# Agent attention and a PReLU feed-forward on one core: the step of a four-copy rounding and the step of one unit's split are changed

## The chip, the core and the metric

The kernel runs on one core of a Trainium2 chip. The metric is the device time of one execution in microseconds; three runs of the kernel before gave 957.25, 957.55 and 958.12 us, so the median is 957.55 us. The core has a matrix engine (TensorE, PE in the rows; PEld is its loading of weights), a vector engine (DVE), a scalar engine (ACT), a general engine (POOL, GpSimd) and a queue that issues DMAs (SP). Each engine works through its own list of instructions in order and waits at a semaphore where another engine's result is needed. PE writes to PSUM; everything else lies in SBUF.

## What is computed

Two batches of 12480 queries, keys and values of width 128 and 49 agents are attended in two stages, and the result goes through a feed-forward with 2048 hidden units:

```
a2k = softmax(scale * agents @ k^T);  agent_v = a2k @ v
q2a = softmax(scale * q @ agents^T);  x = q2a @ agent_v        # 24960 x 128
h = x @ w_in;  g = max(h, 0) + alpha * min(h, 0)
out = g @ w_out
```

Everything is float32 outside. The kernel works in a rounded 32-bit format on PE and splits numbers into a high and a low part (names that end in h and l) to keep the accuracy.

## The kernel before

**Tiling.** The 24960 rows of the output are cut into 52 groups of 480; a group takes 8 steps, so the main loop has 416 steps, numbered from 0. Step s does three things in this order: `g1(s + 2)`, then whatever a plan has put at step s, then `g2(s)`. `g1(s)` makes two blocks of 128 hidden units for its group in PSUM (tile `h`, two buffers: h of step s takes the place of h of step s - 2), as six matmuls in three pairs; ACT then writes `rh = relu(h)`, rounded (line 1077), and DVE writes `rl = relu(h) - rh` (line 1078). `g2(s)` adds these two blocks, times `w_out`, to the group's sum (tile `acc`), as twelve matmuls in six pairs (line 1094). A pair of matmuls works on the two halves of PE's rows side by side. So PE's list can't go past `g1(s + 2)` before DVE has finished `rl` of step s, which reads the buffer that g1(s + 2) overwrites. In the orders below, `rl111` is the `rl` of step 111, and so on; the profile leaves these numbers out.

**The plan.** All other work of the main loop is put at steps by tables of numbers at the head of the file; at one step, work stands in the order in which the code put it in. The scheduler moves nothing: the order written is the order on each engine. Three kinds of such work matter here.

*The query chain.* For each pair of groups, DVE turns the queries (`qt`, line 884), ACT and DVE split them (`qh` 895, `ql` 902), PE makes the logits (921), ACT takes them (`qs`, 929), a DMA swaps the halves (`qw`, 940), DVE adds (947), POOL takes the largest over all partitions (`qm`, a PARTITION_ALL_REDUCE, line 954), DVE subtracts it (959), ACT takes two exponentials (`qmh` 993, `qe` 1001), DVE subtracts them (`qml`, 1005), and POOL sums over all partitions (`qsum`, a PARTITION_ALL_REDUCE of the same 128x960 shape, line 1023, behind a one-column copy called `gate`). The chain repeats every 16 steps: its `qm` is at steps 86, 102, 118 and so on, its `qsum` at 91, 107, 123.

*The second batch's values.* From step 96 on the 25 units of 512 keys of the second batch are worked off, four in 16 steps. For each unit DVE subtracts the largest score (line 676), ACT takes two exponentials (684, 685), DVE subtracts them (690), and `v_split` rounds the values on ACT (666), takes the rest on DVE (667) and sets two columns on POOL (670); PE multiplies two units at a time (`k_av2`, line 708), at the sixth and the tenth of the 16 steps. The table `VALUES` has for each unit four steps: of line 676, of `v_split`, of the exponentials, of line 690. The values' DMA is issued 11 steps before `v_split`.

*The agents of the queries' weight.* `prep_queries(b)` rounds batch b's 49 agents into the weight that the logits of that batch use:

```
nc.scalar.copy(out=aq[c0:c1, h, 0, :], in_=ag[c0:c1, :])      # line 241
nc.scalar.copy(out=aq[r0:r1, h, 0, :], in_=ag[c0:c1, :])      # line 242
nc.vector.tensor_tensor(out=aq[c0:c1, h, 1, :], in0=ag[c0:c1, :],
    in1=aq[c0:c1, h, 0, :], op=ALU.subtract)                  # line 243
nc.gpsimd.tensor_copy(aq[r0:r1, h, 1, :], aq[c0:c1, h, 1, :]) # line 247
```

for two halves h: four casts on ACT, two subtractions on DVE whose two inputs both lie in SBUF, two copies on POOL. `PREPS` has the step for each batch. The second batch's weight has a buffer of its own and is first read by the logits of step 198.

Of the kernel before, what the change touches and what calls it, by code (L numbers as in the profile page):

```python
# [23 lines left out]
    ((1, 2, 3, 4), 6, (12, 13), 14), ((6, 7, 8, 10), 14, (18, 26), 26),  # L24
    ((18, 20, 23, 24), 26, (28, 29), 34), ((28,), 30, (33, 33), 34),
)
VALUES = ((((0, 3, 1, 1), (3, 1, 4, 4)), 6), (((3, 0, 7, 8), (2, 8, 5, 6)), 10))
FOLD = (195, 198, 202, 203)
CHAIN_P = (-18, -16, -16, -14, -13, -13, -11, -10, -7, -6, -5, -5, -5, 1, 10)
POOL_FROM = 2  # L30
# [18 lines left out]
BACK_DVE = (0, 0, 0, 0, 0, 0, 1, 0, 1, 0, 1, 1, 0)  # L49
ALPHA_AT = 6  # L50
WARM = 9
PREPS = (2, 89)
SECOND = (0, 1, 2)
Q_LOAD = -33
K_AHEAD = 13
# [5 lines left out]
def kernel(  # L61
# [1145 lines left out]
    with tc.manual_schedule():  # L1207
# [10 lines left out]
        def at(s, f, *a):  # L1218
            plan.setdefault(s, []).append((f, a))
# [95 lines left out]
        for s, f in zip(EARLY, (lin_sum, *rest)):  # L1315
            at(s, f)
        for b, s in enumerate(PREPS):
            at(s, prep_queries, b)
# [58 lines left out]
        for c, (lo, hi) in enumerate(parts):  # L1377
            s0 = VALUES_FROM + c // len(VALUES) * 16
            steps, av = VALUES[c % len(VALUES)]
            us = list(range(lo, hi))  # L1380
# [59 lines left out]
```

## Time and profile before

| what | us |
|---|---|
| median of three runs | 957.55 |
| lowest and highest run | 957.25, 958.12 |
| the profiled execution: its own time | 957.21 |
| its span, first to last instruction | 955.4 |
| PE busy in the span | 946.9 |
| DVE, ACT, POOL busy | 831.3, 606.1, 233.0 |

The granted clock of PE is 0.999 of full speed over the span, that is the higher of its two levels (2.4 GHz) all through. A row of the trace in order of time has the start and the duration in us, the engine, the line, the operation, the names of what is written and read with their shapes, how many instructions were put together, and, in square brackets, how long the engine sat idle before it and who ended that. Instructions of DVE and ACT overlap by some 0.08 us, the end of one with the start of the next. A matmul's duration is longer than the time after which the next one starts: what counts for PE is the distance between starts.

### The profile page before, as it was taken

What the parts mean: (1) busy time and instruction counts of PE and PEld (TensorE: products, weight loads), DVE (VectorE), ACT (ScalarE), POOL (GpSimd) and SP (SyncE); (2) the same over time, 40 slices, a digit from 0 to 9 for tenths busy, and PEclk for the clock granted to TensorE, in tenths of its full rate; (3) what the DMA queues carried; (4) which work ended last, traced back from release to release, by engine and by line L of the source; (5) the groups of instructions that cost most, each with busy time, mean ns of one, the idle gap of its engine ahead of it and who ended that gap; (6) DMA issues with size and microseconds to landing.
All of it is one profiled execution on the core that took longest, in us unless ns stands there. A gap on an engine that the chain in (4) does not pass through costs nothing.

```text
span 955.4 us, 20984 instructions
## 1 busy us (share of the span) xinstructions
PE 946.9 (99%) x8674; PEld 837.7 (88%) x8674; DVE 831.3 (87%) x1050; ACT 606.1 (63%) x752; POOL 233.0 (24%) x120
## 2 busy tenths in 40 slices
PE   8999999999999999999999999999999999999998
PEld 5678888888889999999888888999999999999997
DVE  7988899999989999999978888878888888888875
ACT  5776666566576776776756566556665656665554
POOL 0001121321332223223123123222313231232220
PEclk9999999999999999999999999999999999999999
DMA  9933636534224324323311311322131223112201
GB/s 346 365 68 64 108 61 115 93 51 78 58 54 105 69 51 97 81 59 81 64 33 32 62 35 32 63 53 45 32 63 41 36 52 64 34 33 43 43 13 32
DMA packets 279569, 69.47 MB, mean 73 GB/s; under 512 B 257183, under 2 KB 272497, under 8 KB 279473
## 3 DMA queue, kind: packets, MB, share of 16 engines
q1 hardware_dynamic: 279329, 68.06, 33.3%
q8 instruction: 68, 1.11, 0.5%
q14 instruction: 28, 0.23, 0.1%
q10 hardware_dynamic: 144, 0.07, 0.0%
HBM read 42.59 MB, written 12.78 MB: 58 GB/s over the span
## 4 chain that ended last, share of the span: by engine, by line
PE 97%; DVE 2%; ACT 0%; issue 0%; DVEq 0%; ACTq 0%
PE acc L1094 57%; PE h L1071 29%; PE lg L921 2%; PE acc L1105 2%; PE av L708 1%; PE kl L614 1%; PE avw L499 1%; PE ktp L398 1%; PE sc L412 1%; DVE red L424 0%; PE warm L211 0%; PE lin_ps L841 0%; PE etp L473 0%; PE a_ps L783 0%; DVE win L324 0%
## 5 line engine op out<-in xcount | busy, mean ns | idle before, releaser
L1077 ACT ACTIVATE rh<-h 128x960 fp32r<-128x960 f32 x416 | 404.1, 972 | 266.5 <-PE h L1071 260.5
L1078 DVE SCALAR_TENSOR_TENSOR rl<-h,rh 128x960 fp32r<-128x960 f32 x416 | 477.9, 1149 | 103.0 <-ACT rh L1077 100.4
L1071 PE MATMUL h<-qmh,sab 64*128 64x480 f32 x1664 | 375.5, 378 | 0.0
L1094 PE MATMUL acc<-rh,wl 64*128 64x480 f32 x1664 | 373.4, 377 | 0.0
L1094 PE MATMUL acc<-rh,wh 64*128 64x480 f32 x1664 | 371.3, 374 | 0.0
L1094 PE MATMUL acc<-rl,wh 64*128 64x480 f32 x1664 | 292.2, 376 | 0.0
L1094 PEld LDWEIGHTS acc<-rh,wl 64*128 64x128 f32 x1664 | 231.6, 184 | 22.8 <-ACT rh L1077 5.8
L1071 PEld LDWEIGHTS h<-qmh,sab 64*128 64x128 f32 x1664 | 232.8, 184 | 17.9 <-DVE rl L1078 1.2
L1094 PEld LDWEIGHTS acc<-rh,wh 64*128 64x128 f32 x1664 | 231.4, 184 | 14.9
L1094 PEld LDWEIGHTS acc<-rl,wh 64*128 64x128 f32 x1664 | 197.9, 184 | 15.1
L1071 PE MATMUL h<-qml,sab 64*128 64x480 f32 x832 | 202.4, 376 | 0.0
L954 POOL PARTITION_ALL_REDUCE qm<-qs x26 | 84.9, 3266 | 375.1 <-DVE qs L947 363.6
L1023 POOL PARTITION_ALL_REDUCE qsum<-qe x24 | 137.9, 5746 | 0.0
L1071 PEld LDWEIGHTS h<-qml,sab 64*128 64x128 f32 x832 | 118.2, 187 | 7.2
L1022 POOL COPY gate<-qml 128x1 f32<-128x1 f32 x24 | 4.5, 189 | 229.5 <-DVE qml L1005 229.5
L1113 ACT COPY os<-acc 128x480 f32<-128x480 f32 x51 | 28.6, 560 | 30.0 <-PE acc L1105 29.5
L993 ACT ACTIVATE qmh<-qs,padb 128x960 fp32r<-128x960 f32 x25 | 27.5, 1099 | 10.5 <-DVE qs L959 9.3
L1173 DVE STREAM_TRANSPOSE ot<-os 128x480 f32<-128x480 f32 x51 | 34.0, 666 | 0.0
L1114 DVE TENSOR_TENSOR os<-acc,os 128x480 f32<-128x480 f32 x51 | 33.2, 650 | 0.2
L1178 DVE TENSOR_TENSOR ot<-ot,qr 128x480 f32<-128x480 f32 x51 | 33.0, 648 | 0.0
L947 DVE TENSOR_TENSOR qs<-qs,qw 128x960 f32<-128x960 f32 x25 | 28.6, 1146 | 1.3 <-DMA qw<-qs 1.3
L959 DVE TENSOR_TENSOR qs<-qs,qm 128x960 f32<-128x960 f32 x25 | 28.7, 1149 | 0.6 <-POOL qm L954 0.5
(185 smaller groups left out, 760.1 us busy)
## 6 DMA issues: line engine op xcount, KB each, us to landing
out_dram<-ot SPq DMA_DIRECT2D x204, 60.0 KB
qin<-in_q_dram SPq DMA_DIRECT2D x200, 60.0 KB
qw<-qs SPq DMA_DIRECT2D x50, 240.0 KB
kw<-in_k_dram SPq DMA_DIRECT2D x12, 512.0 KB
vw<-in_v_dram SPq DMA_DIRECT2D x12, 512.0 KB
kb<-in_k_dram SPq DMA_DIRECT2D x96, 64.0 KB
v<-in_v_dram SPq DMA_DIRECT2D x24, 256.0 KB
win<-in_moe_w_in_dram SPq DMA_DIRECT2D x4, 512.0 KB
```

Of the source, the lines that this page charges most:

```text
L947: nc.vector.tensor_tensor(out=t, in0=t, in1=gq.pop(("w", k)), op=ALU.add)
L954: nc.gpsimd.partition_all_reduce(flat(t), flat(gq["s", k]), P, ReduceOp.max)
L959: nc.vector.tensor_tensor(out=t, in0=t, in1=gq.pop(("m", k)), op=ALU.subtract)
L1023: nc.gpsimd.partition_all_reduce(sums()[:, 0 : 2 * GT], flat(e), P, ReduceOp.add)
L1071: nc.tensor.matmul(h[:, u, 0:GT], lhsT=w[a][r0:r1, m * P : (m + 1) * P], rhs=x[r0:r1, :], start=n == 0, stop=n == 2,)
L1077: nc.scalar.activation(out=rh, in_=h[:, :, 0:GT], func=AF.Relu)
L1078: nc.vector.scalar_tensor_tensor(out=rl, in0=h[:, :, 0:GT], scalar=0.0, in1=rh, op0=ALU.max, op1=ALU.subtract)
L1094: nc.tensor.matmul(acc[:, i, 0:GT], lhsT=a[r0:r1, 2 * m + u, :], rhs=x[r0:r1, u, :], start=m == 0 and n == 0, stop=False,)
L1113: nc.scalar.copy(out=t, in_=acc[:, 0, 0:GT])
L1114: nc.vector.tensor_tensor(out=t, in0=acc[:, 1, 0:GT], in1=t, op=ALU.add)
L1173: nc.vector.transpose(out=t.rearrange("p t i -> p (t i)"), in_=oo.pop(g))
L1178: nc.vector.tensor_tensor(out=t, in0=t, in1=gq.pop(("r", g)).to_broadcast([P, TB, 32]), op=ALU.mult)
```

## The change

Two numbers of two tables.

```
-VALUES = ((((0, 3, 1, 1), (3, 1, 4, 4)), 6), (((3, 0, 7, 8), (2, 8, 5, 6)), 10))
+VALUES = ((((0, 3, 1, 1), (3, 1, 4, 4)), 6), (((3, 2, 7, 8), (2, 8, 5, 6)), 10))
...
-PREPS = (2, 89)
+PREPS = (2, 108)
```

The first moves `v_split` of the third unit of every four from the first to the third of the 16 steps (in six of them: steps 96, 112, 128, 144, 160, 176 become 98, 114 and so on), and its load with it, from 85 to 87 and so on. The second moves the four casts, two subtractions and two copies of `prep_queries(1)` from step 89 to step 108.

**At step 89, on DVE**, between the `rl` of steps 91 and 93 (`aq1` is the queries' weight; L959, 1005 and the like are the query chain). Before:

```order
L1078 SCALAR_TENSOR_TENSOR rl91_3758<-h91_3750,rh91_3757 128x960
L243 TENSOR_TENSOR aq1_3761<-ag1_159,aq1_3761 64x64 x2
L959 TENSOR_TENSOR qs6_3569<-qs6_3569,qm6_3670 128x960
L1078 SCALAR_TENSOR_TENSOR rl92_3791<-h92_3783,rh92_3790 128x960
L1049 STREAM_TRANSPOSE qst5_3794<-qx5_3508 128x32
L1051 TENSOR_SCALAR qr5_3796<-qst5_3794 128x30
L1055 RECIPROCAL qr5_3796<-qr5_3796 128x30
L1078 SCALAR_TENSOR_TENSOR rl93_3821<-h93_3813,rh93_3820 128x960
```

After:

```order
L1078 SCALAR_TENSOR_TENSOR rl91_3758<-h91_3750,rh91_3757 128x960
L959 TENSOR_TENSOR qs6_3569<-qs6_3569,qm6_3668 128x960
L1078 SCALAR_TENSOR_TENSOR rl92_3782<-h92_3774,rh92_3781 128x960
L1049 STREAM_TRANSPOSE qst5_3785<-qx5_3508 128x32
L1051 TENSOR_SCALAR qr5_3787<-qst5_3785 128x30
L1055 RECIPROCAL qr5_3787<-qr5_3787 128x30
L1078 SCALAR_TENSOR_TENSOR rl93_3812<-h93_3804,rh93_3811 128x960
```

The two subtractions of `aq1` are gone from in front of L959; the rest stands as it did. On ACT, the four casts that stood between `rh91` and `rh92` are gone in the same way.

**At step 108, on DVE**, from the query chain's last subtraction to the `rl` of step 112. Before:

```order
L1005 TENSOR_TENSOR qml7_4351<-qe7_4349,qmh7_4306 128x960
L1078 SCALAR_TENSOR_TENSOR rl110_4376<-h110_4368,rh110_4375 128x960
L1173 STREAM_TRANSPOSE ot12_4379<-os12_4232 128x480
L1078 SCALAR_TENSOR_TENSOR rl111_4401<-h111_4393,rh111_4400 128x960
L1078 SCALAR_TENSOR_TENSOR rl112_4426<-h112_4418,rh112_4425 128x960
```

After:

```order
L1005 TENSOR_TENSOR qml7_4342<-qe7_4340,qmh7_4297 128x960
L1078 SCALAR_TENSOR_TENSOR rl110_4367<-h110_4359,rh110_4366 128x960
L243 TENSOR_TENSOR aq1_4370<-ag1_159,aq1_4370 64x64 x2
L1173 STREAM_TRANSPOSE ot12_4379<-os12_4223 128x480
L1078 SCALAR_TENSOR_TENSOR rl111_4401<-h111_4393,rh111_4400 128x960
L1078 SCALAR_TENSOR_TENSOR rl112_4426<-h112_4418,rh112_4425 128x960
```

The two subtractions now stand behind `rl110` and in front of `ot12` (the turn of a finished group) and `rl111`. On ACT the four casts stand between `rh110` and `rh111`.

**At step 108, on POOL**, between the sum and the next largest value of the query chain. Before:

```order
L1022 CAST gate7_4353<-qml7_4351 128x1
L1023 ISA qsum_1289<-qe7_4349 128x960
L670 MEMSET v2_1_6_4488 128x4x2
L670 MEMSET v2_1_5_4523 128x4x2
L670 MEMSET v2_1_4_4592 128x4x2
L954 ISA qm8_4680<-qs8_4576 128x960
```

After:

```order
L1022 CAST gate7_4344<-qml7_4342 128x1
L1023 ISA qsum_1289<-qe7_4340 128x960
L247 COPY aq1_4370<-aq1_4370 64x64 x2
L670 MEMSET v2_1_5_4519 128x4x2
L670 MEMSET v2_1_6_4559 128x4x2
L670 MEMSET v2_1_4_4592 128x4x2
L954 ISA qm8_4678<-qs8_4576 128x960
```

The two copies of `aq1` stand behind `qsum` of the same 16 steps. The columns of units 5 and 6 are set in the other order, since their splits have changed places.

**At steps 112 to 115, on DVE**, the same place in all six: the query chain's `ql`, and the splits `v2` of units 6 and 5. Before:

```order
L902 TENSOR_TENSOR ql8_4485<-qt8_4429,qh8_4483 128x960
L676 TENSOR_TENSOR s1_1213<-s1_1213,kmax1_1216 128x196
L667 TENSOR_TENSOR v2_1_6_4488<-v1_6_4130,v2_1_6_4488 128x4x128
L1078 SCALAR_TENSOR_TENSOR rl115_4515<-h115_4507,rh115_4514 128x960
L1178 TENSOR_TENSOR ot12_4379<-ot12_4379,qr6_4303 128x480
L690 TENSOR_TENSOR e2_1_4_4519<-s1_1213,e2_1_4_4519 128x4x49
L667 TENSOR_TENSOR v2_1_5_4523<-v1_5_4179,v2_1_5_4523 128x4x128
L1078 SCALAR_TENSOR_TENSOR rl116_4547<-h116_4539,rh116_4546 128x960
L676 TENSOR_TENSOR s1_1213<-s1_1213,kmax1_1216 128x196
L1078 SCALAR_TENSOR_TENSOR rl117_4589<-h117_4581,rh117_4588 128x960
```

After:

```order
L902 TENSOR_TENSOR ql8_4485<-qt8_4429,qh8_4483 128x960
L676 TENSOR_TENSOR s1_1213<-s1_1213,kmax1_1216 128x196
L1078 SCALAR_TENSOR_TENSOR rl115_4511<-h115_4503,rh115_4510 128x960
L1178 TENSOR_TENSOR ot12_4379<-ot12_4379,qr6_4294 128x480
L690 TENSOR_TENSOR e2_1_4_4515<-s1_1213,e2_1_4_4515 128x4x49
L667 TENSOR_TENSOR v2_1_5_4519<-v1_5_4168,v2_1_5_4519 128x4x128
L1078 SCALAR_TENSOR_TENSOR rl116_4543<-h116_4535,rh116_4542 128x960
L667 TENSOR_TENSOR v2_1_6_4559<-v1_6_4206,v2_1_6_4559 128x4x128
L676 TENSOR_TENSOR s1_1213<-s1_1213,kmax1_1216 128x196
L1078 SCALAR_TENSOR_TENSOR rl117_4589<-h117_4581,rh117_4588 128x960
```

The split of unit 6 has moved past `rl115` and `rl116`. On ACT its cast moves in the same way, from in front of `rh115` to between `rh116` and the copy `qs8` (line 929). On SP its load now stands behind the eight loads of queries that it used to precede.

## Rows read from the trace of the kernel before

**Rows 1.** The page: busy us of each engine, share of the span, instructions.

```profile
PE 946.9 (99%) x8674; PEld 837.7 (88%) x8674; DVE 831.3 (87%) x1050; ACT 606.1 (63%) x752; POOL 233.0 (24%) x120
```

**Rows 2.** Waits from 255 to 300 us: who for whom, us, times, longest.

```profile
PEld h L1071 <- DVE rl L1078: 0.6, 2, 0.3
```

**Rows 3.** Instructions in order of time around step 89: ACT, DVE, POOL.

```profile
266.09 0.23 ACT L241 CAST aq<-ag 64x64 fp32r<-64x64 f32 x1
...
267.18 0.97 ACT L1077 ACTIVATE rh<-h 128x960 fp32r<-128x960 f32 x1
268.99 1.10 ACT L993 ACTIVATE qmh<-qs,padb 128x960 fp32r<-128x960 f32 x1 [0.84 <-DVE qs L959]
...
267.30 0.46 DVE L243 TENSOR_TENSOR aq<-ag,aq 64x64 fp32r<-64x64 f32 x2
267.79 1.16 DVE L959 TENSOR_TENSOR qs<-qs,qm 128x960 f32<-128x960 f32 x1
...
270.98 1.16 DVE L1078 SCALAR_TENSOR_TENSOR rl<-h,rh 128x960 fp32r<-128x960 f32 x1 [0.25 <-ACT rh L1077]
...
267.65 1.41 POOL L247 CAST aq<-aq 64x64 fp32r<-64x64 f32 x2 [4.05 <-DVE aq L243]
```

**Rows 4.** PE in order of time where it starts g1(95).

```profile
272.19 0.49 PE L1071 MATMUL h<-qmh,sab 64*128 64x480 f32 x2
272.52 0.38 PE L1071 MATMUL h<-qml,sab 64*128 64x480 f32 x2
272.73 0.38 PE L1071 MATMUL h<-qmh,sab 64*128 64x480 f32 x2
```

**Rows 5.** DVE, ACT and PEld in order of time, steps 112 to 116.

```profile
318.17 0.69 DVE L667 TENSOR_TENSOR v<-v,v 128x512 fp32r<-128x512 f32 x1
318.77 1.15 DVE L1078 SCALAR_TENSOR_TENSOR rl<-h,rh 128x960 fp32r<-128x960 f32 x1
...
321.28 1.15 DVE L1078 SCALAR_TENSOR_TENSOR rl<-h,rh 128x960 fp32r<-128x960 f32 x1
...
321.47 0.97 ACT L1077 ACTIVATE rh<-h 128x960 fp32r<-128x960 f32 x1 [0.19 <-PE h L1071]
...
322.48 0.19 PEld L1071 LDWEIGHTS h<-qmh,sab 64*128 64x128 f32 x2 [0.15 <-DVE rl L1078]
```

**Rows 6.** DVE, POOL, ACT and PE in order of time, steps 107 to 111.

```profile
307.76 1.15 DVE L1078 SCALAR_TENSOR_TENSOR rl<-h,rh 128x960 fp32r<-128x960 f32 x1
308.83 0.67 DVE L1173 STREAM_TRANSPOSE ot<-os 128x480 f32<-128x480 f32 x1
309.48 1.16 DVE L1078 SCALAR_TENSOR_TENSOR rl<-h,rh 128x960 fp32r<-128x960 f32 x1
...
308.06 5.74 POOL L1023 PARTITION_ALL_REDUCE qsum<-qe  x1
...
308.47 0.97 ACT L1077 ACTIVATE rh<-h 128x960 fp32r<-128x960 f32 x1 [0.93 <-PE h L1071]
...
311.50 0.41 PE L1071 MATMUL h<-qmh,sab 64*128 64x480 f32 x2
```

**Rows 7.** Line 690 alone (ns, least, median, most); DVE and POOL around 295 us.

```profile
L690 DVE TENSOR_TENSOR e<-s,e x25: 246/353/934, 285.3 to 473.9; 128x196 fp32r<-128x196 f32 x24, 96x98 fp32r<-96x98 f32 x1
...
295.72 0.93 DVE L690 TENSOR_TENSOR e<-s,e 128x196 fp32r<-128x196 f32 x1
...
294.66 3.04 POOL L954 PARTITION_ALL_REDUCE qm<-qs  x1 [15.30 <-DVE qs L947]
```

**Rows 8.** Line 297 alone, its ordinary calls and the one during line 954.

```profile
L297 DVE TENSOR_SCALAR mag_win<-mag_win x4: 418/424/428, 10.2 to 23.0; 128x512 f32<-128x512 f32 x4
...
L297 DVE TENSOR_SCALAR lin<-lin x1: 2007/2007/2007, 46.8 to 46.8; 128x512 f32<-128x512 f32 x1
```

**Rows 9.** Busy us of each engine, granted clock, DMA share and GB/s, 312 to 320 us.

```profile
312.00:320.00 8.00, 8.00 (x78) 7.86 (x76) 7.58 (x10) 6.47 (x10) 1.93 (x4) 1.00 0.01 2
```

## The prediction

> **What bounds the kernel now.** The page comes first: PE is busy for 946.9 of 955.4 us [rows 1], so a change can bring only what PE loses at a wait, and cost only a new wait of PE. The starts of PE's pairs are read next: undisturbed pairs follow each other after 0.21 us (272.52 to 272.73 in [rows 4]), nine pairs make a step of some 1.9 us, and that is the floor. Then the waits of PE in the stretch that the change touches: from 255 to 300 us one kind stands out, g1 waiting twice for `rl` of DVE, 0.6 us in total [rows 2]. So the question at each place of the change is whether `rl` of step s is done when PE wants to start g1(s + 2). Last, since the two subtractions move to a step in which POOL works, the rows of DVE's two-input instructions beside POOL's reduces [rows 7, 8]. The granted clock is 1.00 in this part [rows 9], so no term needs it.
>
> The sum is made against the profiled execution, 957.21 us (span 955.4 and 1.8 around it); the median of the runs shown is 0.34 higher, 957.55, and the forecast is given on that. 0.2%, or 1.9 us, is about what a measurement of this kernel can tell from no change: faster means below 955.63, slower above 959.47.
>
> **Step 89, eight instructions removed.** On ACT the four casts run from 266.09 until `rh92` starts at 267.18, 1.09 us; on DVE the two subtractions take 267.30 to 267.79, 0.49 us [rows 3]. ACT then waits 0.84 us for the chain's subtraction (L959) before its exponential, `rl93` waits another 0.25 us for `rh93` behind that exponential, and starts at 270.98 [rows 3]; it ends at 270.98 + 1.16 = 272.14, and g1(95) starts at 272.19 [rows 4]. There the first pair takes 0.33 us instead of 0.21 (272.19 to 272.52 in [rows 4]), 0.12 us lost, and some 0.04 in front of it; g1(96) loses about as much, which makes the two waits of [rows 2] some 0.3 us of PE's time. Without the subtractions L959 starts 0.49 us earlier and everything behind it that waits for it with it, which covers 0.16 us twice. Gain 0.3, with 0 and 0.6 (the whole of the waits) as ends. The two copies on POOL, 1.41 us [rows 3], waited for nobody's sake there.
>
> **The third unit's split, six times.** Its subtraction takes 318.17 to 318.77, 0.60 us of DVE, and stands ahead of `rl115` and `rl116` (318.77 and 321.28); PE's weights for g1(118) waited 0.15 us for the latter, which ended at 322.43 [rows 5]. Moved behind `rl116`, that `rl` ends 0.6 us earlier and this wait goes. Only two of the six places show more than a few hundredths of it; in the others nothing is to be had. What is late next: on ACT the cast, 0.6 us, now stands between `rh116` and the copy of the logits, and `rh117`, which had 0.19 us of idle time in front of it [rows 5], starts some 0.4 us later at most; `rl117` waits for that by about 0.1 us, since DVE does the moved split meanwhile. PE wants g1(119) a whole step after g1(118), so that is covered; if the cover were gone it would cost 0.1 us in each of six places. I take a gain of 0.1 us in all, between a loss of 0.6 and a gain of 0.3. The load is issued behind the eight loads of queries, two steps later, and the split reads it two steps later, so it has the same 11 steps; the DMA engines are nearly idle (0.01) when it is due [rows 9]. No cost. The two settings of columns on POOL that change places are first read by `k_av2`, four or eight steps on. No cost.
>
> **Step 108, eight instructions added.** On ACT four casts, 1.09 us, go into the 0.93 us in which ACT sat idle before `rh111` at 308.47 [rows 6]: `rh111` 0.1 to 0.2 us later, covered because DVE comes to `rl111` only at 309.48 or later. On POOL the two copies stand behind `qsum` (308.06 to 313.80 [rows 6]); the next work there with a due time is the columns for step 118, and the weight is read only at step 198. No cost. On DVE two subtractions, 0.49 us, stand ahead of `ot12` and `rl111`. Alone they would put `rl111` from 309.48 to 309.97, its end to 311.13; PE starts g1(113) at 311.50 [rows 6]. Covered, with 0.37 us to spare.
>
> But they don't run alone. `qsum` starts on POOL at 308.06, and the first of them would start at about 308.83, when `rl110` ends [rows 6]. DVE instructions that came while a reduce ran on POOL show what can happen: line 690, also with two inputs in SBUF, takes 353 ns as a rule and 934 at most; that one started at 295.72, 1.06 us after a `qm` reduce of 3.04 us had started at 294.66 [rows 7]. It behaves as if it had been let in at 295.72 + 0.93 - 0.35 = 296.30, that is 1.65 us after the reduce's start and 1.4 before its end. Line 297 gives the same picture: 2007 ns instead of 424 beside the first reduce [rows 8]. No row of the kernel has a two-input DVE instruction inside a `qsum` reduce, so when `qsum` would let the subtraction in must be bounded. If it is let in at time R, then the first ends at R + 0.21, the second at R + 0.46, `ot12` takes 0.65 us until `rl111` starts and that 1.16: `rl111` ends at R + 2.3, PE restarts 0.05 us later and loses 0.1 us on its first pair as in [rows 4], so PE loses R + 2.45 - 311.50. The bounds: never held up, loss 0. Let in 1.65 us after the start as with `qm`, whose operand has the same shape: R = 309.71, loss 0.66. Let in after the same share of the reduce, 1.65/3.04 of 5.74 us: R = 311.18, loss 2.1. Let in 1.4 us before the end, as with `qm` counted from there: R = 312.4, loss 3.35. Only at the end: R = 313.80, loss 4.75. I take the first of the held cases, 0.66: the reading of the same 128x960 operand is the part that both reduces share, and the extra 2.7 us of the sum are more likely in what comes after it. This is an estimate, and the weakest step.
>
> The rule of the Trainium skill for this (SBUF — State Buffer, "Who interferes with whom") is that a DVE instruction with two SBUF inputs and a GpSimd instruction that reads SBUF need the same read interface, and that whoever starts first keeps it for its whole instruction. The rows agree that there is a hold-up, and disagree on its length, since line 690 got in 1.4 us before the reduce's end. By the rule the loss would be the last of the bounds, not the one I take.
>
> **Sum.** -0.3 - 0.1 + 0.66 = +0.26 us: 957.5 on the profiled execution, 957.8 on the median.
>
> **The rivals.** *No hold-up.* The two subtractions are as small as at step 89 (64 partitions, 64 columns) and slip through. Speaks for it that no `qsum` is seen to hold anything; against it line 690. Then -0.4: 957.15. *Hold-up by share of the reduce.* Speaks for it that the sum takes 5.74/3.04 times as long on the same operand, which could be its loop over the input; -0.4 + 2.1: 959.25, just inside no change. *Hold-up until late*, the rival on the other side: `rl111` comes so late that PE stands for over 3 us at g1(113), at step 111, once. -0.4 + 3.35: 960.5, slower. It decides from R = 311.35 on, where the loss passes 2.3 us and the sum 1.9. *Held to the end of `qsum`*: -0.4 + 4.75: 961.9. It is what the rule named above would do here; the rows with line 690 speak against it. *The change doesn't do what it says*: the orders show that it does, so this gets nothing.
>
> **How the numbers follow.** Forecast (let in as with `qm`, around 957.8) 0.48; by share (959.25, give or take 0.4) 0.25; until late (960.5) 0.14; to the end (961.9) 0.05; no hold-up (957.15) 0.05; else (the split's cover gone in six places, something not seen) 0.03. Faster by over 0.2% needs 1.9 us of gain, where all waits seen here come to less than 1: 0.03. Slower: 0.14 + 0.05, four tenths of the 0.25 and a little of the rest, 0.30. Within 0.2%: 0.67. The range starts at 956.9, under the case without a hold-up, and ends at 960.2, which takes in the case by share and the early part of the late one; the late end and beyond, some 0.17, stay out.
>
> **What would show each step.** In the profile after, g1(95) and g1(96) start without the wait for `rl`, and `rl93` starts some 0.4 us earlier against its neighbours. The wait of 0.15 us for `rl116` is gone. Line 243 at about 308.5 us is the row that decides: two instructions of 0.2 us each, or the first one long; its start plus its duration less 0.21 is R. Behind it stands a gap of PEld before g1(113), released by DVE `rl`, of the size of the loss, and one such place only. The prediction is wrong if line 243 is short, if it is over 2.5 us, or if PE waits at the steps 112 to 122 for `rl117` or `rl118`, for then the split's new place costs what I put at nothing.

## The result: 962.31 us, slower by 0.52%

After: 962.31 us, the median of 6 runs (961.36 to 964.02). Before, in runs taken beside them: 957.75 (6 runs, 956.71 to 958.16). The ratio is 1.0052 [1.0042 to 1.0062], so the change makes the kernel slower, by about 4.6 us; the forecast was 957.8, with 960.2 as the top of its range.

The page of the kernel after, busy time of each engine: all five do what they did in [rows 1], within 4.1 us, while the span grew from 955.4 to 960.4. Hardly any work was added; it was waited for, or done slowly.

```profile
span 960.4 us, 20983 instructions
...
PE 948.4 (99%) x8674; PEld 841.8 (88%) x8674; DVE 834.7 (87%) x1050; ACT 605.7 (63%) x752; POOL 232.4 (24%) x120
```

**Step 89** went as forecast. The waits from 255 to 300 us (who for whom: us, times, longest) have no line any more in which PEld waits for `rl`, the one of [rows 2]; what is left of the chain's delay there is ACT's wait:

```profile
ACT qmh L993 <- DVE qs L959: 0.3, 1, 0.3
```

DVE in order of time shows why, against [rows 3]: line 959 starts as soon as `rl91` is done.

```profile
266.70 1.16 DVE L1078 SCALAR_TENSOR_TENSOR rl<-h,rh 128x960 fp32r<-128x960 f32 x1 [0.81 <-ACT rh L1077]
267.78 1.15 DVE L959 TENSOR_TENSOR qs<-qs,qm 128x960 f32<-128x960 f32 x1
268.84 1.15 DVE L1078 SCALAR_TENSOR_TENSOR rl<-h,rh 128x960 fp32r<-128x960 f32 x1
```

**Step 108** is where the time went. Line 243 alone (durations: least, median, most, in ns), then DVE, POOL and ACT in order of time, against [rows 6] (start us, duration us, engine, line; in brackets the idle time ahead of it and what ended it):

```profile
L243 DVE TENSOR_TENSOR aq<-ag,aq x4: 211/222/3853, 72.5 to 312.6; 64x64 fp32r<-64x64 f32 x4
```

```profile
307.64 1.15 DVE L1078 SCALAR_TENSOR_TENSOR rl<-h,rh 128x960 fp32r<-128x960 f32 x1
308.71 4.11 DVE L243 TENSOR_TENSOR aq<-ag,aq 64x64 fp32r<-64x64 f32 x2
312.85 0.68 DVE L1173 STREAM_TRANSPOSE ot<-os 128x480 f32<-128x480 f32 x1
313.45 2.18 DVE L1078 SCALAR_TENSOR_TENSOR rl<-h,rh 128x960 fp32r<-128x960 f32 x2
...
308.24 5.75 POOL L1023 PARTITION_ALL_REDUCE qsum<-qe  x1 [0.26 <-ACT aq L241]
314.06 0.53 POOL L247 CAST aq<-aq 64x64 fp32r<-64x64 f32 x2
...
308.10 0.24 ACT L242 CAST aq<-ag 64x64 fp32r<-64x64 f32 x1
308.35 0.97 ACT L1077 ACTIVATE rh<-h 128x960 fp32r<-128x960 f32 x1
```

The two subtractions, 0.46 us when alone, take 4.11 us, and the first of them 3.85 of these. With the reading of the prediction (end of the two, less 0.46) they were let in at 308.71 + 4.11 - 0.46 = 312.36 us: 4.12 us after `qsum` had started at 308.24, and 1.63 before its end at 313.99 (4.11 or 4.12 us behind its start in e1, e6 and e7 below). `rl111`, on which g1(113) waits, starts at 313.45 instead of 309.48. PE in order of time at that place:

```profile
310.92 0.64 PE L1094 MATMUL acc<-rl,wh 64*128 64x480 f32 x4
314.62 0.49 PE L1071 MATMUL h<-qmh,sab 64*128 64x480 f32 x2 [3.06 <-DVE rl L1078]
314.95 0.38 PE L1071 MATMUL h<-qml,sab 64*128 64x480 f32 x2
315.17 0.38 PE L1071 MATMUL h<-qmh,sab 64*128 64x480 f32 x2
315.38 0.38 PE L1094 MATMUL acc<-rh,wl 64*128 64x480 f32 x2
315.60 0.49 PE L1094 MATMUL acc<-rh,wh 64*128 64x480 f32 x2
315.89 0.60 PE L1094 MATMUL acc<-rh,wl 64*128 64x480 f32 x2
316.29 0.60 PE L1094 MATMUL acc<-rh,wh 64*128 64x480 f32 x2
```

The wait of 3.06 us isn't all. From 315.89 on the pairs follow each other after 0.40 us instead of 0.22. The windows of the kernel after, around that place (window, length, then busy us and count of PE, PEld, DVE, ACT, POOL; then the granted clock, the share of the DMA engines and GB/s), against [rows 9]:

```profile
310.90:314.60 3.70, 0.66 (x7) 0.25 (x3) 3.64 (x5) 0.37 (x1) 3.57 (x5) 1.00 0.00 0
314.60:316.00 1.40, 1.38 (x12) 1.18 (x14) 1.40 (x2) 0.41 (x1) 0.10 (x3) 0.90 0.13 23
316.00:320.00 4.00, 4.00 (x28) 3.37 (x25) 2.41 (x3) 1.58 (x3) 0.00 (x0) 0.61 0.00 0
320.00:330.00 10.00, 10.00 (x96) 9.10 (x94) 9.44 (x15) 8.73 (x14) 0.00 (x0) 1.00 0.33 74
```

The clock column reads 0.61 from 316 to 320 us, so TensorE ran at the lower of its two levels (1.2 of 2.4 GHz) for the larger part of that stretch, right behind the one long wait of PE. PE counts as busy there, which is most of why its busy time grew by 1.5 us.

**Where the 4.5 us lie, step by step.** From PE's rows I took the start of the last matmul of each g1(s), and from it the length of each step less that of the same step before. In the table: us; the last column is the whole from step 84 to 198, which leaves out the start of the program. There PE waits for the first loads, and the profiled executions of the kernels differ by -0.3 to +1.3 us; of the span's 5.0 us, 0.5 come from there.

| kernel | g1(95), (96) | g1(102), (118) | g1(113) | g1(114), (115) | g1(123) to (187) | 84 to 198 |
|---|---|---|---|---|---|---|
| after | -0.30 | -0.43 | +3.33 | +1.56 | +0.43 | +4.49 |
| e1, agents alone | -0.30 | 0 | +3.74 | +2.19 | 0 | +5.51 |
| e2, split alone | 0 | -0.43 | 0 | 0 | +0.39 | -0.11 |
| e7, PE filled | -0.30 | -0.43 | +3.60 | 0 | +0.42 | +3.16 |
| e8, one column | 0 | 0 | +2.99 | +0.98 | 0 | +3.82 |
| e4, agents at 110 | -0.30 | -0.42 | 0 | 0 | +0.43 | -0.46 |

g1(107) is left out of the columns: it moves by -0.16 to +0.07 in kernels that change nothing ahead of it (e8, e11).

In e1 and e8 the column g1(113) is not the wait alone: there the granted clock is down before PE starts again. PE of e1 in order of time, then one of its windows (length, PE's busy us and count, clock, DMA share, GB/s):

```profile
314.12 0.77 PE L1071 MATMUL h<-qmh,sab 64*128 64x480 f32 x2 [3.05 <-DVE rl L1078]
314.68 0.60 PE L1071 MATMUL h<-qml,sab 64*128 64x480 f32 x2
```

```profile
310.00:314.00 4.00, 1.07 (x9) 0.88 0.00 0
```

PE starts again at 314.12, and the window that ends at 314 already has 0.88 (e8 has 0.98 from 310 to 315, ahead of its start at 315.12). The first two pairs take 0.56 and 0.40 us, where after has 0.33 and 0.22, so 0.41 us of e1's 3.74 are the clock's, and of e8's 2.99 as well (0.57 and 0.39). Without them e1's wait costs 3.33 us, as in after, and the lower clock costs 2.60 us in e1, 1.39 in e8 and 1.56 in after.

### The profile page after: what moved, and what is told of

The parts are those of the page before. It is cut to its first block, busy times and chain, and to the rows that moved or that the text cites. A ratio compares the mean times of both kernels' runs of the same rounds, so it can differ in the third digit from the quotient of the medians.

```text
span 960.4 us, 20983 instructions
## 1 busy us (share of the span) xinstructions
PE 948.4 (99%) x8674; PEld 841.8 (88%) x8674; DVE 834.7 (87%) x1050; ACT 605.7 (63%) x752; POOL 232.4 (24%) x120
## 4 chain that ended last, share of the span: by engine, by line
PE 96%; DVE 2%; DMA 1%; ACT 1%; issue 0%; DVEq 0%; ACTq 0%
PE acc L1094 56%; PE h L1071 28%; PE lg L921 2%; PE acc L1105 2%; PE av L708 1%; PE kl L614 1%; DMA kw<-in_k_dram 1%; PE avw L499 1%; PE ktp L398 1%; PE sc L412 1%; PE etp L473 0%; DVE aq L243 0%; PE warm L211 0%; PE lin_ps L841 0%; PE a_ps L783 0%
## 5 line engine op out<-in xcount | busy, mean ns | idle before, releaser
L1094 PEld LDWEIGHTS acc<-rh,wl 64*128 64x128 f32 x1664 | 235.5, 185 | 23.5 <-ACT rh L1077 5.8
L1071 PEld LDWEIGHTS h<-qmh,sab 64*128 64x128 f32 x1664 | 235.7, 184 | 19.3 <-DVE rl L1078 4.0
L1094 PEld LDWEIGHTS acc<-rh,wh 64*128 64x128 f32 x1664 | 235.0, 184 | 14.3
L1094 PEld LDWEIGHTS acc<-rl,wh 64*128 64x128 f32 x1664 | 200.0, 184 | 14.7
L884 DVE STREAM_TRANSPOSE qt<-qin 128x960 f32<-128x960 f32 x25 | 29.1, 1166 | 0.0
```

Source lines behind the costliest of these rows:

```text
L884: nc.vector.transpose(out=flat(t), in_=gq.pop(("in", k)).rearrange("p h t i -> p (h t i)"))
L1071: nc.tensor.matmul(h[:, u, 0:GT], lhsT=w[a][r0:r1, m * P : (m + 1) * P], rhs=x[r0:r1, :], start=n == 0, stop=n == 2,)
L1094: nc.tensor.matmul(acc[:, i, 0:GT], lhsT=a[r0:r1, 2 * m + u, :], rhs=x[r0:r1, u, :], start=m == 0 and n == 0, stop=False,)
```

## The experiments

My theory after the result: the subtraction, because it has two inputs in SBUF, is kept out by `qsum` until shortly before that ends; PE's wait for it costs 3.3 us, and the lower clock that follows the wait costs 1.6 more. Against it stand: the split's new place makes it; the queue on ACT or POOL makes it; it is held to the reduce's end; it is held the same time from the start of any reduce; the lower clock comes of something else.

### One half at a time: e1 and e2

e1 is before with the agents' move alone; e2 is after with that move undone.

```
e1:  -PREPS = (2, 89)      e2:  -PREPS = (2, 108)
     +PREPS = (2, 108)          +PREPS = (2, 89)
```

> Only the rounding of the agents moves to step 108; the third unit's split stays where it was. Theory (the first subtraction is held up by the sum on POOL until about 4.1 us after the sum's start, PE waits over 3 us at g1(113) and runs at its lower clock for some 3.5 us behind the wait): line 243 has one instruction of about 3.8 us, the median is 4.6 to 5.2 us above the kernel before. Rival (the split's new place costs too, and the two together make the loss): under 3 us above the kernel before.

> Only the third unit's split moves; the agents are rounded at step 89 as before. Theory: no wait of PE over 0.3 us anywhere in steps 84 to 200, the median within 0.6 us of the kernel before, the profile's loss of PE at g1(102) and g1(118) gone (0.2 us each). Rival (the split in its new place holds up rl117 or the exponentials' differences): 1 us or more above.

e1: 962.47 beside 957.37, 1.0056 [1.0043 to 1.0070]. e2: 957.66 beside the same, 1.0001 [0.9992 to 1.0010]. The whole loss is the agents' move. In e1 line 243 again takes up to 3845 ns and PE waits 3.05 us at g1(113), as in after; that the loss is a microsecond larger there comes from the lower clock, which sets in earlier. The split alone is nearly even: it gains 0.43 us at g1(102) and g1(118) and gives 0.39 back in steps of 0.07 to 0.18 nine steps behind the later splits.

### The same work two steps on, and before the chain: e4 and e3

```
-PREPS = (2, 108)
+PREPS = (2, 110)     e4
+PREPS = (2, 88)      e3
```

> The split moved as in the change, the agents rounded at step 110, so that the two subtractions stand behind rl112 and come about 4.4 us after the sum's start, when POOL still works on it for over 1 us. Theory (the sum lets others in 1.6 us before its end): both of line 243 take 0.2 to 0.3 us, no wait of PE over 0.3 us, the median within 0.8 us of the kernel before. Rival (held to the end of the sum, as the Trainium skill has it on the page SBUF — State Buffer): line 243 over 1.2 us, rl113 a microsecond later, PE waits 0.5 to 1.2 us.

> The split moved as in the change, the agents rounded at step 88, where DVE sits idle for 0.81 us and ACT for 1.00 us and no reduce runs on POOL. Theory: both of line 243 take 0.2 us, PE has no wait at g1(95) and g1(96), the median 0.2 to 0.9 us below the kernel before, too little to be told from it with certainty. Rival (it is the number of instructions that has to go somewhere): no gain against the kernel before.

e4: 956.97 beside 957.37, 0.9994 [0.9985 to 1.0003]. It is the run that tells the end of the hold from the end of the reduce. DVE and POOL of e4 in order of time:

```profile
312.02 0.46 DVE L243 TENSOR_TENSOR aq<-ag,aq 64x64 fp32r<-64x64 f32 x2
...
307.88 5.75 POOL L1023 PARTITION_ALL_REDUCE qsum<-qe  x1 [0.26 <-issue]
```

The subtractions start 4.14 us after `qsum`, while it runs on for 1.6 us, and take their 0.46 us. So `qsum` doesn't hold them to its end: an instruction that comes 4.14 us in isn't held at all.

e3: 957.18, 1.0001 [0.9992 to 1.0009]. Step 89's wait for `rl` is gone with one step's move as well, the subtractions are short, and from step 84 to 198 the kernel gains 0.39 us, as e4 gains 0.46. Neither is told from before by the times. By the steps e4 is the best of the versions that leave nothing out; the times don't settle it.

### Without inputs, with one, and with one column: e5, e11 and e8

e5 is after with the second batch's subtractions replaced by a write of as many elements; e8 and e11 are before with one small DVE instruction more at step 108.

```
 e5
+            if b:
+                nc.vector.memset(aq[c0:c1, h, 1, :].bitcast(F32), 0.0)
...
 e8
+            t = p2.tile([P, 1], F32, tag="none", name="touch")
+            nc.vector.tensor_tensor(
+                out=t, in0=padb, in1=ident[:, 0:1], op=ALU.add
+            )
...
+        at(108, touch)
...
 e11, as e8 but
+            nc.vector.tensor_scalar(
+                out=t, in0=padb, scalar1=1.0, scalar2=None, op0=ALU.add
+            )
```

> The changed kernel, with the second batch's two subtractions replaced by two settings to zero of the same 64x64 places (so the low part of its queries' weight is left out); casts, copies, steps and waits are the same. Theory (the hold-up is for the input from SBUF, not for room on DVE or the casts on ACT): the two settings take 0.1 to 0.3 us each during the sum, PE has no wait of 3 us, the median within 0.8 us of the kernel before. Rival (DVE and ACT have no room there for eight more instructions, or any DVE instruction that uses SBUF there is held): 2 us or more above.

> As e8_one_column, but the added instruction adds a constant to one column, so it has one input in SBUF and not two. Theory (the second input is what is kept out): 0.1 to 0.2 us, PE has no wait of 2 us. Rival (any DVE instruction that reads SBUF there is kept out, or this form is too): 3.4 us again and the time 4 to 5 us above.

> The kernel before, with one DVE addition of one column added at step 108 behind rl110 (two inputs in SBUF, 128x1, into a tile that nobody reads); nothing else is moved. Theory (what counts is that a two-input instruction comes while the sum reads, not its size): it takes about 3.8 us, PE waits 2.7 to 3.3 us at g1(113) and the lower clock follows, the median 4.0 to 5.0 us above the kernel before. Rival (the hold-up grows with the subtractions' work): it takes 0.1 to 0.2 us, the median within 0.5 us.

e5: 957.53 beside 957.11, 1.0001 [0.9992 to 1.0010]. e11: 957.56 in one run, beside a median of 957.46. e8: 960.78 beside 957.11, 1.0036 [1.0022 to 1.0050]. DVE in e5, then in e11, then in e8, with the `qsum` of each:

```profile
309.11 0.29 DVE L244 MEMSET aq<- 64x64 f32 x2
...
308.59 5.75 POOL L1026 PARTITION_ALL_REDUCE qsum<-qe  x1 [0.26 <-issue]
```

```profile
309.12 0.14 DVE L1322 TENSOR_SCALAR touch<-padb 128x1 f32<-128x1 f32 x1
...
308.35 5.75 POOL L1023 PARTITION_ALL_REDUCE qsum<-qe  x1
```

```profile
309.95 3.48 DVE L1322 TENSOR_TENSOR touch<-padb,ident 128x1 f32<-128x1 f32 x1
...
309.18 5.74 POOL L1023 PARTITION_ALL_REDUCE qsum<-qe  x1
```

All three start within 0.8 us of `qsum`'s start. Without an input, 0.29 us for both; with one, 0.14; with two, 3.48 us for a single column, until 4.25 us after the reduce's start. That is a little less than expected (3.8 us, and 4.0 to 5.0 in the median, where 3.7 were measured), because this one comes 0.77 us into the sum and not 0.47. The casts and the POOL copies of e5 stand where they stand in after, so neither queue makes the loss. Of two-input instructions a single column is held as 64x64 are.

e11 differs from e8 in the operation too (TENSOR_SCALAR for TENSOR_TENSOR). Two rows of the kernel before, DVE and POOL, show that the operation isn't it:

```profile
85.55 0.65 DVE L1114 TENSOR_TENSOR os<-acc,os 128x480 f32<-128x480 f32 x1
...
84.72 3.04 POOL L954 PARTITION_ALL_REDUCE qm<-qs  x1 [11.51 <-DMA qin<-in_q_dram]
```

This TENSOR_TENSOR has one input in PSUM (`acc`) and one in SBUF; it comes 0.83 us into a `qm`, ahead of the 1.65 us after which line 690 got in, and takes its usual 0.65 us. So it is the second SBUF input that is held here. That one SBUF input always goes through is not shown: line 297 [rows 8] has one, of 128x512, and was slow beside a reduce.

### Another reduce in the same place: e9

After, with `qsum` as a maximum, so that the sums are left out.

```
-            nc.gpsimd.partition_all_reduce(sums()[:, 0 : 2 * GT], flat(e), P, ReduceOp.add)
+            nc.gpsimd.partition_all_reduce(sums()[:, 0 : 2 * GT], flat(e), P, ReduceOp.max)
```

> The changed kernel with POOL's reduce behind the query chain taking the largest value instead of the sum (so the sums of the second stage's softmax are left out and the output's scale is not the reference's); operand, place and waits are the same. Theory (the reduce keeps others out for its own length but for the last 1.4 to 1.6 us, so the kind of reduce sets it): the reduce takes 3.0 to 3.3 us, line 243 has one instruction of 1.0 to 1.5 us, PE waits 0.3 to 0.9 us at g1(113), the clock stays 1.00; 1.5 us below to 1 us above the kernel before. Rival (a fixed hold-up for the 128x960 operand, whatever the operation): 3.8 us again.

One run, 959.01 beside a median of 957.46, 0.55 us above the range that I had given; 1.3 us of it lie at the start of the program, and steps 84 to 198 lose 0.45. DVE and POOL in order of time, then, in a fence of its own, the waits from 300 to 325 us (who for whom: us, times, longest):

```profile
309.56 1.64 DVE L243 TENSOR_TENSOR aq<-ag,aq 64x64 fp32r<-64x64 f32 x2
...
309.08 3.05 POOL L1023 PARTITION_ALL_REDUCE qsum<-qe  x1 [0.26 <-ACT aq L241]
```

```profile
PEld h L1071 <- DVE rl L1078: 1.0, 1, 1.0
```

The maximum takes 3.05 us on the operand on which the sum takes 5.75, and the subtractions are let in at 309.56 + 1.64 - 0.46 = 310.74: 1.66 us after its start, 1.39 before its end. That is the 1.65 and 1.4 us that the prediction read from `qm` [rows 7], now with this kernel's own subtraction. So the sum holds 4.11 us because it is a sum; nothing in DVE's instruction differs. The hold is neither the same time nor the same share of both reduces (0.54 of the maximum, 0.72 of the sum). g1(113) loses 0.87 us here, and PE's clock stays at 1.00.

### One step on and one step back: e6 and e10

```
-PREPS = (2, 108)
+PREPS = (2, 109)     e6
+PREPS = (2, 107)     e10
```

> The changed kernel with the agents rounded at step 109: the first subtraction comes about 2.5 us after the sum's start and not 0.6. Theory (let in 4.1 us after the sum's start whenever it came): line 243 has one instruction of 1.7 to 2.1 us, rl112 ends at about 1.2 us after its time, PE waits 0.4 to 0.9 us at g1(114), too short for the lower clock; the median 0.2 below to 1.0 us above the kernel before. Rival (a fixed time that any hold-up takes): 3.8 us again, and 4 to 5 us above.

> The split moved as in the change, the agents rounded one step earlier, at 107: the two subtractions stand in front of the chain's last subtraction, and the sum on POOL can start only behind that. Theory: both of line 243 take 0.2 us, PE has no wait over 0.6 us, the median from 0.8 us below to 0.8 above the kernel before: one step is worth over 4 us. Rival (there is no room for half a microsecond of DVE around these steps): 1.5 us or more above.

e6: 958.28 beside 957.11, 1.0008 [0.9998 to 1.0017]. e10: 958.16 beside 957.46, 1.0004 [0.9994 to 1.0013]. DVE and POOL of e6, and its waits from 300 to 325 us:

```profile
309.65 2.38 DVE L243 TENSOR_TENSOR aq<-ag,aq 64x64 fp32r<-64x64 f32 x2
...
307.46 5.75 POOL L1023 PARTITION_ALL_REDUCE qsum<-qe  x1 [0.26 <-issue]
```

```profile
PEld h L1071 <- DVE rl L1078: 0.8, 2, 0.5
```

They start 2.2 us into `qsum` instead of 0.5, and are let in at 309.65 + 2.38 - 0.46 = 311.57, again 4.11 us after its start: the moment belongs to the reduce and not to the arrival. DVE loses 1.9 us there instead of 3.65, with `ot12` and `rl111` done ahead of it; PE's weights wait 0.5 us at the longest, and the clock stays at 1.00 from 310 to 325 us. Line 243 is held a little longer than expected, and the median is 1.2 us above before, 0.2 over the range; by the steps it is 0.56. In e10 they are done before `qsum` begins and are short (0.46 us for both), but the casts stand ahead of the chain's exponential on ACT, `qml` waits 0.50 us for that, and g1(112) is 0.50 us late.

### PE kept at work during the wait: e7

After, with 14 matmuls more ahead of the wait, on data that nobody reads.

```
+FILL = 14
...
+        def fill():
+            t = pair_tile("fill")
+            for i in range(FILL):
+                nc.tensor.matmul(
+                    t[:, i % 2, :], lhsT=wh[:, 0, :],
+                    rhs=wh[:, 0:4, :].rearrange("p f d -> p (f d)"), start=True, stop=True,
+                )
+
+        at(110, fill)
```

> The changed kernel with 14 more matmuls of 512 columns in front of g2(110), into a tile that nobody reads (3.0 us of work for PE where it would stand). The hold-up is as before. Theory (1.6 us of the loss are the lower clock behind PE's wait): PE waits under 0.6 us at g1(113), the granted clock stays 1.00 from 310 to 322 us, the median 2.6 to 3.8 us above the kernel before instead of 4.6 to 5.1. Rival (the slow pairs behind the wait come from something else, such as the backlog of DVE): the same 4.6 to 5.1, or more with the added work.

961.43 beside 957.11, 1.0041 [1.0026 to 1.0056]. PE of e7 in order of time, then its windows (length, PE's busy us and count, clock, DMA share, GB/s):

```profile
310.66 3.45 PE L1324 MATMUL fill<-wh 128*128 128x512 f32 x14
314.04 0.49 PE L1095 MATMUL acc<-rh,wl 64*128 64x480 f32 x2
314.37 0.38 PE L1095 MATMUL acc<-rh,wh 64*128 64x480 f32 x2
314.59 0.38 PE L1095 MATMUL acc<-rh,wl 64*128 64x480 f32 x2
```

```profile
310.00:315.00 5.00, 5.00 (x30) 1.00 0.01 3
315.00:320.00 5.00, 5.00 (x48) 1.00 0.02 3
```

Line 244 of e7 (243 of after) is held as long as before, 4.09 us for the two, and step 113 is 3.60 us longer; but the clock stays at 1.00 and steps 114 and 115 cost nothing. So the lower clock came of PE's standing still, and its price is the table's 1.56 us. The median is 4.3 us above that of before, more than I had expected, and only 0.2 less than in after: the profiled execution lost 1.0 us at the start of the program, and four runs don't settle a difference of this size. The filling is also longer than the wait: `rl111` is done at 315.03, and g1(113) starts at 315.46, so step 113 costs 3.60 us and not 3.33. What shows that the clock is the cause is the steps, not the medians, and the granted clock over the span: 0.999 or 1.000 in all four runs of e7, 0.995 to 0.998 in the six of after.

## Why the prediction was wrong

- **What bounds the kernel, and where to look:** held. PE's waits decide; line 243 was the row that decided, and the gap of PEld behind it stood in one place, g1(113).
- **Step 89, gain 0.3:** 0.30 us, 0.12 at g1(95) and 0.18 at g1(96). The two POOL copies cost nobody anything.
- **The split, gain 0.1:** e2 gives 0.11 in all, but not by the terms named, so the agreement is luck. The weights of g1(118) no longer wait (0.21 us gained; the row of PEld below, against [rows 5]) and g1(102) gains as much; then 0.39 is lost in pieces at g1(123), (139), (155), (171) and (187), nine steps behind the splits from the second on, where I had put the cover as whole. The waits of after from 320 to 500 us name the place, the weights of a new `acc`; before had the first line once, with 0.2 us, and the second not at all. Which of the moved instructions makes PE late there no run tells.

```profile
326.94 0.18 PEld L1071 LDWEIGHTS h<-qmh,sab 64*128 64x128 f32 x1
```

```profile
PEld acc L1094 <- issue: 0.8, 4, 0.2
PEld acc L1094 <- ACT os L1113: 0.4, 1, 0.4
```

- **Step 108, casts, copies and the two subtractions as such:** held. e4 and e5 have them at that part of the program with no loss. One thing was missed: `qsum` starts 0.45 us behind the start of `gate` in after and 0.15 in before, and so it is in every version run here: 0.44 or 0.45 with the copies of `aq` behind the sum, 0.15 or 0.16 without. So the sum came 0.3 us later; why, no run tells.
- **The moment at which `qsum` lets the subtraction in:** this is the step that failed. I had bounds of 0, 0.66, 2.1, 3.35 and 4.75 us and took 0.66, on the ground that both reduces read the same operand and the sum's extra 2.7 us come after that. They don't: the extra time is held as well (e9: 1.66 us of 3.05 as a maximum; after, e1, e6 and e7: 4.1 of 5.75 as a sum). The right bound was "until late", counted from the end: 1.4 us before it by the bound, 1.63 as measured, and the loss at g1(113) 3.35 as worked out, 3.33 as measured. That these two agree so closely is chance: the sum stood 0.3 us later, and let the subtraction in 0.2 us earlier against its own end. This bound had a chance of 0.14, the one that I took more than three times as much, on an argument that no row bore out. The rows of before spoke against the case that I took. My reading rests on the one call of line 690 beside a `qm` of 3.04 us; five more calls came into longer ones, of 3.31 or 3.32 us, and took 0.87 or 0.88 us, and line 297 [rows 8] came into the first. One of the five and line 297, each with its reduce, in the kernel before:

```profile
365.25 0.87 DVE L690 TENSOR_TENSOR e<-s,e 128x196 fp32r<-128x196 f32 x1
...
363.86 3.31 POOL L954 PARTITION_ALL_REDUCE qm<-qs  x1 [14.96 <-DVE qs L947]
```

```profile
46.81 2.01 DVE L297 TENSOR_SCALAR lin<-lin 128x512 f32<-128x512 f32 x1
...
46.31 3.69 POOL L954 PARTITION_ALL_REDUCE qm<-qs  x1
```

Read in the prediction's way, line 690 got in at 365.25 + 0.87 - 0.35 = 365.77, 1.91 us after the start of its reduce and 1.40 before the end; line 297 at 46.81 + 2.01 - 0.42 = 48.40, 2.09 after and 1.60 before. Over reduces of 3.04, 3.31 and 3.69 us the time from the start grows with the reduce, from 1.65 to 2.09, and the time to the end stays at 1.4 to 1.6. So line 297 doesn't give "the same picture" as the first call, as the prediction has it, and the forecast's case was ruled out for `qm` already. Between "until late" and "by share" these rows don't decide (0.54 to 0.58 of each reduce); the sum does, with 0.72. What ends the hold at that point, no run tells.
- **The rule of the Trainium skill** (SBUF — State Buffer, "Who interferes with whom", and for the whole instruction "SBUF: two separate sides"), that a DVE instruction with two SBUF inputs and a GpSimd instruction that reads SBUF shut each other out, whoever is first, for the whole instruction: that two inputs are shut out, and none or one of 128x1 not, agrees with e5, e8 and e11, and that the reduce keeps it longer than I took agrees too; how long doesn't. The runs have the end of the hold 1.63 us (sum) and 1.39 us (maximum) ahead of the instruction's end, and e4 has subtractions of ordinary length in that last part.
- **The lower clock:** a term that the prediction lacks. It says that the granted clock is 1.00 in this part, so that no term needs it; that was true of the kernel before, which had no such wait there. It cost 1.56 us, and by it the result is above even the "until late" rival's 960.5: -0.30 and -0.43 of gains, +3.33, +1.56 and +0.43, give +4.59; the trace has +4.49, with -0.10 at g1(107).

## What to carry to other kernels

Before a two-input VectorE instruction is moved, see which GpSimd reduce runs at its new place, and price it as held until shortly before the end of that reduce, however small it is; two steps later cost nothing here, and one step later some 0.9 us of PE's steps (e6, from g1(114) to g1(120), the split's gain aside). When a reading has two origins (so long after the start, so long before the end), look for a row with another length before you weigh them; here the trace of the kernel before had six, and they spoke against the reading from the start. And price a wait of PE of 2 to 3 us with what the clock takes as well, 1.4 to 2.6 us here.

## What the runs showed of the hardware that I had not expected

- The reduce across partitions of 128x960 takes 5.75 us as a sum and 3.05 as a maximum, and keeps two-input DVE instructions out for 4.11 and 1.66 us of these: whether they come 0.5 (after), 0.8 (e8) or 2.2 us (e6) behind its start, and whether they have 64x64 elements or 128x1.
- Of PE's waits in this full stretch, those of 3.06 us (after), 3.05 (e1) and 2.3 (e8) went with the lower clock, which cost 1.56, 2.60 and 1.39 us; one of 0.6 us (e9) did not. The same wait had two prices: in after the clock was still at 1.00 when PE started again and fell behind that, in e1 it was down before.
